# A fused block-causal attention and gated FFN kernel: the second batch's v loads ahead of the casts of w_out, a new order in tiles 0 to 2, and the last tile's stores on two queues

## The chip, the cores and the metric

The kernel runs on one core of a Trainium2 chip. The time is the device time of one execution in microseconds (us); lower is better. Before the change the median of three runs is 353.19 us (352.29 to 354.38).

The core's engines run their own instruction streams in program order: PE multiplies matrices, DVE (VectorE) and ACT (ScalarE) work element by element, POOL (GpSimd) does that too and here issues the loads that change the type on the way, and SP (SyncE) only issues transfers. Semaphores order the engines among each other.

## The reference

```python
# q, k, v: (8 batches, 8 heads, 576 positions, 64); blocks of 64 positions
scores = q @ k.T / sqrt(64)          # per batch and head
scores = where(block(i) >= block(j), scores, -1e9)
attn = softmax(scores) @ v
x = attn, as 4608 tokens x 512       # heads side by side
gate = maximum(x @ w_gate, 0)        # 512 x 1536
out = (gate * (x @ w_val)) @ w_out   # 1536 x 512, result float32
```

## The kernel before, in words

**Tiles.** The FFN runs in nine tiles of 512 tokens: tile j below 8 holds the first 512 positions of batch j, and tile 8 the last 64 positions ("tails") of all eight. A tile multiplies x by w_gate and w_val (L1193; 96 matmuls), ACT applies the maximum (L1204), DVE multiplies the two (L1214), and the result goes through w_out: in tiles 0 and 1 by 48 plain matmuls (L1298), from tile 2 on by seven products of half blocks (`seven_products`, L891), for which POOL forms sums of w_out's blocks (`weight_sums`, acts W0 to W5). In the last tiles a similar scheme serves the first stage too (L1063).

**Attention** runs in rounds: round r = 4b + p handles heads 2p and 2p + 1 of batch b, so rounds 4 to 7 are the second batch's. A round has the scores (act `s4`; L552), the exponentials on ACT (`e4`; L557), zeros for the masked corners (`c4`), the products with v for its two heads (`a4` and `b4`; ten L687 matmuls each), and the transpose of the result into the FFN's x (`x4`; L730). For the tails there are acts `S`, `L`, `E`, `A` and `B` by batch.

**Order.** PE's stream is the FFN's generator, `ffn_gen`, which yields once per matmul. All else is an "act" with a name and a place in the table `AT`, counted in yields of the FFN: 0 to 95 is the first stage of tile 0, 96 to 143 its w_out, 144 on tile 1, 288 on tile 2. The end of the kernel sorts the acts by place, runs the FFN up to each place, and then issues the act:

```python
for n in sorted(acts, key=lambda n: AT[n]):
    at = int(place_of(AT[n]))
    ffn(at - place[0])
    place[0] = max(place[0], at)
    acts[n]()
```

No scheduler moves anything after that, so the order in the table is the order on every engine. The table's base stands at L1454, and blocks of `AT.update` further down replace places. `HOW` (from L1687) says which engine does what.

**The second batch's entry.** q, k and v come by these acts, and all of them share POOL, SP and the transfers' bandwidth with the load of w_out:

- SP loads q and k of four heads at a time in float32 (`E1q0`, then `E1q4` for q and `E1q6` for k of heads 4 to 7; `load_wide`, L164), and w_out in six pieces of 512 KB (`w00` to `w21`; `load_w`, L458).
- POOL casts q and k to bf16 (`q0`, `q4`, `q6`; L174) and most of w_out (`cw00` to `cw21/0`; L484). The last pieces of w_gate and w_val are cast by `cg21`, `cv21/0` and `cv21/1` in the same way.
- v is loaded by POOL's queue with the cast on the way: `E1v0` to `E1v3`, two heads each, two transfers each (`load_v_casting`, L186; the DMA at L183). Before the change, POOL's order was: `cg21`, `cv21/0`, `q0`, `E1v0`, the six w_out casts, `E1v1`, `q4`, `q6`, `E1v2`, `E1v3`.
- PE transposes q and k of heads 4 to 7 in act `m2` (`pe_wide`, 8 + 8 matmuls at L367), and ACT or DVE copies them out by head pair (`m2`, `m3`). Round 6 needs this.
- The third batch's q and k come over a DMA transpose and are put in order by `u0` to `u3` (`unpermute`, L330); its v by `E2v0` to `E2v3`.

**Stores.** A tile's result is kept in blocks of 256 columns and stored by `put_block`. In the last tile each block is two transfers, i = 0 and 1 (L773); its four blocks come in the order (0,0), (1,256), (0,256), (1,0), the last in two halves p0 = 0 and 1, where the first number is the half of the batches and the second the first column.

Of the kernel before, what the change touches and what calls it, by code (L numbers as in the profile page):

```python
# [17 lines left out]
def kernel(  # L18
# [10 lines left out]
    nc = tc.nc  # L29
# [729 lines left out]
    def put_block(j, hi, n0, ob, p0, p1):  # L759

        n = slice(n0, n0 + 256)
        rows = ob.rearrange("q (p n) -> q p n", n=256)
        if j < B:
            r0 = S * j + 256 * hi + 128 * p0
            (nc.scalar if j < UPS - 1 else nc.sync).dma_start(
                out[r0 : r0 + 128 * (p1 - p0), n].rearrange("(p q) n -> q p n", q=128),
                rows,
            )
        else:
            by_batch = out.rearrange("(b s) n -> b s n", b=B)  # L770
            for i in range(2):
                b0 = 4 * hi + 2 * p0 + i
                ((nc.scalar, nc.sync)[i] if (hi, n0) == (1, 0) else nc.sync).dma_start(  # L773
                    by_batch[b0 : b0 + 2 * (p1 - p0) - 1 : 2, 512:576, n].rearrange(
                        "b s n -> s b n"
                    ),
                    rows[64 * i : 64 * i + 64],
                )
# [91 lines left out]
    def seven_products(j, quads, sums, late_up=None, head=None):  # L870
# [42 lines left out]
        def store_later(hi, n0, ob, p0=0, p1=2):  # L913
            if store:
                store.pop()()
            if j < B:
                store.append(lambda: put_block(j, hi, n0, ob, p0, p1))
            else:
                put_block(j, hi, n0, ob, p0, p1)
# [440 lines left out]
    dve, act, pool = nc.vector.tensor_copy, nc.scalar.copy, nc.gpsimd.tensor_copy  # L1360
# [7 lines left out]
    with tc.manual_schedule(engines={E.PE, E.DVE, E.Activation, E.Pool, E.SP}):  # L1368
# [4 lines left out]
        def round_at(r, how):  # L1373

            exps = []

            def begin():
                exps.extend(visit(r))
                exps[0]()
                exps[1]()  # L1380

            corner, first, second, xT = how
            return {
                f"s{r}": begin,
                f"e{r}": lambda: exps[2](),
                f"c{r}": lambda: corners(r, zeros_by[corner]),
                f"a{r}": lambda: head_av(r, 0, first),
                f"b{r}": lambda: head_av(r, 1, second),
                f"x{r}": lambda: (
                    to_xT_pe(r, by[xT[0]], xT[1]) if xT else to_xT_dma(r)  # L1390
                ),
            }
# [53 lines left out]
        def mains_1(hp):  # L1446
# [7 lines left out]
        AT = {  # L1454
            "Lq0": -63.5,
            "Lq2": -62.27,
            "Lv0": -61.59,
            "Lv2": -59.5,
            "Lq6": -59.5,
            "Lq4": -59.5,  # L1460
            "v00": -58.48,
            "g00": -56.5,
# [224 lines left out]
        HOW = {  # L1687
            "t0": ("act", "dve"),
            "t1": ("dve", "dve"),
            "m0": (("act", "dve"), ("sc", "ffn")),  # L1690
            "m1": (("dve", "act"), None),
            "m2": (("act", "act"), ("sc", "ffn")),
            "m3": (("act", "act"), None),
            "u0": ("pool", "pool"),
            "u1": ("dve", "dve"),
# [95 lines left out]
                "cv00/23": "pool",  # L1791
            }
        )
        STEADY = {"s": 2, "e": 8, "c": 15, "a": 22, "b": 26, "x": 26.1}
        acts = {
            "Lq0": lambda: e0.load_qk(0, 2, nc.scalar),
# [85 lines left out]
        for b in range(4, B):  # L1882
            base = 144 * (b - 1)
            for i in range(4):
                r = 4 * b + i
                here = ("sc", "sc") if i == 3 else ("one", "ffn")
                acts.update(round_at(r, ("dve", *here, None)))
                for n, p in STEADY.items():
                    AT[f"{n}{r}"] = base + 28 * i + p + (5 if i == 3 and n in "abx" else 0)
# [17 lines left out]
        for c in range(6):  # L1907
# [268 lines left out]
                "cg00/23": -17.37,  # L2176
                "c3a": -3.24,
                "cg01/23": 4.15,
            }
        )  # L2180
        assert set(acts) == set(AT), set(acts) ^ set(AT)
# [43 lines left out]
```

## Time and profile before

| | |
|---|---|
| median of three runs | 353.19 us (352.29 to 354.38) |
| the profiled execution's own time | 352.44 us |
| its span in the profile | 350.7 us |
| time outside the span | 1.74 us |
| w_out loads: issue to landing, median | 10.6 us |
| busy share POOL, ACT, DVE | 51%, 57%, 60% |

How to read it: the profile comes from one execution, whose span is the time from its first to its last recorded instruction; the execution's own time is 1.74 us more. Engines are shown as PE (matmuls), PEld (PE's loads of weights), DVE, ACT, POOL and SP; an ending "q" stands for the issue of transfers. A line such as "L687" is a line of the kernel. In a timeline a row is a run of like instructions with its start and length, and in brackets the idle time just before it and what ended it. The chain of waits follows the work that ended last back to what released it, and so names one releaser where several may have come at nearly the same time. A row of a window holds the busy time of the engines in that stretch, the granted clock of PE, the busy share of the transfer engines and the rate in GB/s. Landing is when a transfer's data are there.

### The profile page before, as it was taken

The page shows a single profiled execution, that of the slowest core. Times are in us where ns is not written, and L with a number is a line of the kernel's source. Part 1 is how long each engine was busy: PE and PEld are TensorE (multiplying, and loading weights), DVE is VectorE, ACT ScalarE, POOL GpSimd, SP SyncE. Part 2 cuts the span into 40 slices and gives each one's busy share as a digit, 9 for nine tenths or more (in the row PEclk, how much of TensorE's full clock was granted, in tenths as well). Part 3 has the DMA queues.
Part 4 walks back from the last instruction along what each step waited for, and adds up shares of the span by engine and source line. Part 5 has one row for each costly group of instructions (what it writes and reads, how often), then busy time and mean ns, then how long its engine had stood idle before and what let it go on. Part 6 is the DMA issues. An engine that isn't in the chain of part 4 may idle for free.

```text
span 350.7 us, 8432 instructions
## 1 busy us (share of the span) xinstructions
PE 341.3 (97%) x3317; PEld 216.4 (62%) x3317; DVE 210.4 (60%) x541; ACT 200.3 (57%) x323; POOL 178.2 (51%) x216
## 2 busy tenths in 40 slices
PE   7899999999999999999999999999999999999994
PEld 3544445555554568555855576556755598888883
DVE  4654435557538675466636762666456757787783
ACT  4942776888336672666365555655366627725731
POOL 4836798799709910690029209950490042711630
PEclk9999999999999999999999999999999999999999
DMA  8999999999989999999449953999410012003005
GB/s 243 294 354 374 348 269 176 136 92 145 161 199 104 133 172 176 136 148 165 73 111 139 136 114 112 132 141 147 119 47 15 17 49 96 3 3 119 2 3 120
DMA packets 155624, 48.40 MB, mean 138 GB/s; under 512 B 134592, under 2 KB 152000, under 8 KB 155584
## 3 DMA queue, kind: packets, MB, share of 16 engines
q0 software_dynamic: 83776, 10.49, 57.8%
q1 hardware_dynamic: 65872, 30.68, 39.5%
q10 hardware_dynamic: 5936, 6.69, 6.1%
q8 instruction: 26, 0.43, 0.6%
q14 instruction: 14, 0.11, 0.1%
HBM read 37.75 MB, written 9.44 MB: 135 GB/s over the span
## 4 chain that ended last, share of the span: by engine, by line
PE 83%; DMA 10%; DVE 2%; ACT 2%; POOL 1%; issue 0%; SPq 0%; POOLq 0%; DVEq 0%
PE ffnp L1193 36%; PE ffnp L891 12%; PE upa L1063 6%; PE one L891 5%; DMA stage<-in_moe_w_val_dram 5%; PE ffnp L1298 4%; DMA stage<-in_moe_w_out_dram 3%; PE sc L552 3%; PE upc L1063 3%; PE ffnp L687 2%; PE one L552 2%; DMA v_bf<-in_v_dram 2%; ACT attnT L516 2%; PE ffnp L1063 1%; PE one L687 1%; PE sc L687 1%
## 5 line engine op out<-in xcount | busy, mean ns | idle before, releaser
L1214 DVE TENSOR_TENSOR hT<-gate_sb,ffnp 128x512 bf16<-128x512 bf16 x82 | 55.9, 683 | 60.7 <-ACT gate_sb L1204 31.7
L1193 PE MATMUL ffnp<-xT,wv 128*128 128x512 bf16 x328 | 90.0, 379 | 0.0
L1193 PE MATMUL ffnp<-xT,wg 128*128 128x512 bf16 x316 | 86.4, 379 | 0.0
L1204 ACT ACTIVATE gate_sb<-ffnp 128x512 bf16<-128x512 f32 x79 | 48.2, 613 | 41.9 <-PE ffnp L1193 41.7
L557 ACT ACTIVATE attnT<-sc 128x1024 bf16<-128x1024 f32 x56 | 57.7, 1047 | 0.0
L1193 PEld LDWEIGHTS <-wv 128*128 128x128 bf16 x336 | 30.2, 98 | 33.6 <-issue 3.0
L1193 PEld LDWEIGHTS <-wg 128*128 128x128 bf16 x336 | 30.8, 98 | 32.2 <-issue 2.2
L439 POOL DMA_DIRECT2D q_bf<-in_q_dram x20 | 17.7, 900 | 37.8 <-DVE hT L1214 36.8
L923 ACT COPY ob<-ffnp 128x512 f32<-128x512 f32 x21 | 12.3, 586 | 41.9 <-PE ffnp L891 40.4
L891 PEld LDWEIGHTS <-stage 128*128 128x128 bf16 x336 | 32.5, 98 | 3.7
L687 PEld LDWEIGHTS <-attnT 128*128 128x128 bf16 x640 | 26.9, 98 | 12.4 <-issue 1.5
L439 POOL DMA_DIRECT2D v_bf<-in_v_dram x30 | 24.3, 879 | 10.7 <-DVE stage L802 10.1
L891 PEld LDWEIGHTS <-hT 128*128 128x128 bf16 x252 | 24.1, 98 | 4.6 <-DVE hT L1095 0.7
L1298 PE MATMUL ffnp<-wo,hT 128*128 128x512 bf16 x96 | 23.8, 379 | 0.0
L564 ACT ACTIVATE attnT<-one 128x512 bf16<-128x512 f32 (+1 forms) x28 | 15.1, 540 | 14.7 <-PE ffnp L552 14.6
L552 PEld LDWEIGHTS <-kTm 64*128 64x128 bf16 x384 | 13.0, 94 | 14.2 <-issue 9.0
L891 PE MATMUL ffnp<-wo,hT 128*128 128x256 bf16 x168 | 21.5, 273 | 0.1
L891 PE MATMUL ffnp<-stage 128*128 128x256 bf16 x168 | 21.3, 273 | 0.0
L439 POOL DMA_DIRECT2D k_bf<-in_k_dram x20 | 18.0, 944 | 0.0
L848 DVE TENSOR_TENSOR stage<-hT 128x512 bf16<-128x512 bf16 (+1 forms) x45 | 17.5, 393 | 0.5
L552 PE MATMUL sc<-qTm,kTm 64*128 64x512 bf16 (+1 forms) x168 | 17.7, 305 | 0.0
L1099 POOL TENSOR_TENSOR hT<-attnT,gate_sb 128x512 bf16<-128x512 f32 x4 | 4.6, 1159 | 25.1 <-ACT gate_sb L1107 25.1
(186 smaller groups left out, 628.9 us busy)
## 6 DMA issues: line engine op xcount, KB each, us to landing
out_dram<-ob ACTq DMA_DIRECT2D x24, 256.0 KB, 2.4
stage<-in_moe_w_val_dram SPq DMA_DIRECT2D x6, 512.0 KB, 8.2
stage<-in_moe_w_gate_dram SPq DMA_DIRECT2D x6, 512.0 KB, 8.6
stage<-in_moe_w_out_dram SPq DMA_DIRECT2D x6, 512.0 KB, 10.6
q_bf<-in_q_dram POOLq DMA_DIRECT2D x20, 128.0 KB, 4.6
k_bf<-in_k_dram POOLq DMA_DIRECT2D x20, 128.0 KB, 5.8
v_bf<-in_v_dram POOLq DMA_DIRECT2D x20, 128.0 KB, 6.2
stage<-in_q_dram SPq DMA_DIRECT2D x4, 512.0 KB, 10.1
```

The source lines that it names most:

```text
L439: ins = nc.gpsimd.dma_start(dst, part_of)
L552: nc.tensor.matmul(o, kTm[b % 2][head_of(hh), c, hp, :], qT, start=True, stop=True)
L557: return lambda: nc.scalar.activation(at[:, :, lo : lo + 512], sc, AF.Exp, scale=scale)
L564: nc.scalar.activation(at[:, hh, 1024 : 1024 + w], third[hh][:, 0:w], AF.Exp, scale=scale)
L687: nc.tensor.matmul(av[:, p, :], at[:, col : col + 128], v_bf[b % 2][:, c, h, :], start=(p == 0), stop=(c == p), skip_group_check=True,)
L848: ins = (eng or nc.vector).tensor_tensor(out=s(i), in0=a, in1=b, op=op)
L891: nc.tensor.matmul(to, sums.of(c)[which]()[:, 128 * p : 128 * p + 128], right, start=first, stop=(c == 5), skip_group_check=True,)
L1063: nc.tensor.matmul(to[:, 256 * f : 256 * f + 256], left(which, u // 2)[:, kc, lo : lo + 128], right[which](kc), start=new and (f, kc) == ( ...
L1193: ins = nc.tensor.matmul(to, (wg, wv)[t][f // 4][:, c, 128 * (f % 4) : 128 * (f % 4) + 128], x[:, c], start=(c == 0), stop=(c == 3),)
L1204: nc.scalar.activation(gate_sb, gate, AF.Relu)
L1214: nc.vector.tensor_tensor(out=h, in0=gate_sb, in1=val, op=AX.mult)
L1298: ins = nc.tensor.matmul(op, hT[f][:, 128 * s : 128 * (s + 1)], wo[f // 4][:, f % 4, n0:n1], start=(f == 0), stop=(f == 11),)
```

## The change

- In `put_block`, the last tile's transfers are given out anew: block (0,0) and the second half of (1,0) wholly to SP, of the others i = 0 to SP and i = 1 to ACT. SP issues seven instead of eight, ACT three instead of two.
- In `HOW`, the copies of `u0` and `u1`, which were on POOL and ACT, DVE and POOL, go to DVE and ACT, DVE and DVE, and `cw21/1` from ACT to DVE.
- In `AT`, some ninety places are new. On the engines this comes to:
  - POOL: `cv21/0` ahead of `cg21`; `E1v0` and `E1v1` both ahead of the w_out casts (`E1v2` and `E1v3` stay behind `q6`); the tails' loads `T0` ahead of `T1`; the third batch's v in the order of heads 6 and 7, 2 and 3, 4 and 5, 0 and 1, in a row (before: 2, 3, 0, 1, 6, 7, 4, 5 with a copy of `u1` between); the second `weight_sums` ahead of the load `l3`.
  - PE: `s4` two places later and `s5` one earlier; `m2` ahead of `b4` and `a4`, which before stood ahead of it, and `b4` ahead of `a4`; in tile 1 the tail products `A1` behind `s8`, the tail acts `S2` and `L2` of the third batch some places earlier, `x11` later; the others by one or two places.
  - SP: the DMA transpose `dq3` ahead of `x8`.

The diff, cut to the edits that these lines speak of:

```diff
-                ((nc.scalar, nc.sync)[i] if (hi, n0) == (1, 0) else nc.sync).dma_start(
+                (nc.scalar if i and (hi, n0) != (0, 0) and not p0 else nc.sync).dma_start(
...
+        HOW.update(
+            {
+                "cw21/0": "pool",
+                "cw21/1": "dve",
+                "t0": ("act", "dve"),
+                "u0": ("dve", "act"),
+                "u1": ("dve", "dve"),
+            }
+        )
...
+                "E1v1": 32.255,
+            }
+        )
+        AT.update(
+            {
+                "E1q0": 30.6,
...
+                "cv21/0": 32.13,
+                "w21": 34.31,
+                "E1q6": 34.34,
+                "E1q4": 34.34,
+                "cg21": 34.35,
+                "q0": 34.39,
+                "E1v0": 35.95,
+                "E1v1": 35.95,
+                "cw00": 36.0,
+                "cw01": 36.0,
+                "cw10": 36.01,
+                "cw11": 36.03,
+                "cw21/0": 36.05,
+                "cw20": 36.05,
+                "E2q4": 37.3,
+                "q4": 41.12,
+                "cv20": 44.31,
+                "q6": 48.64,
+                "E1v2": 88.39,
+                "s4": 96.02,
...
+                "T0": 108.36,
...
+                "s5": 115.76,
...
+                "T1": 119.45,
+                "m2": 122.13,
+                "E0v": 122.62,
+                "b4": 122.95,
+                "a4": 123.23,
...
+                "m3": 125.27,
+                "s6": 128.0,
...
+                "b5": 130.73,
...
+                "E2v3": 177.42,
+                "E2v2": 178.09,
+                "E2v1": 178.09,
+                "S1": 181.62,
+                "E2v0": 182.84,
+                "s8": 199.54,
+                "e8": 200.02,
+                "A1": 202.39,
+                "W1": 205.95,
+                "l3": 206.44,
...
+                "b8": 215.84,
...
+                "dq3": 246.36,
+                "e11": 246.48,
+                "a10": 248.52,
+                "x8": 249.37,
...
+                "S2": 269.46,
+                "W5": 271.62,
+                "L2": 279.14,
+                "x11": 280.4,
...
```

More of the change, by code (lines that the diff above doesn't have):

```diff
@@ L2178 @@
                 "cg01/23": 4.15,
+                "E1v1": 32.255,
[4 more added lines that the diff above has]
+                "E1q0": 30.6,
+                "w01": 30.61,
+                "w00": 30.76,
+                "w11": 30.82,
+                "w20": 30.83,
+                "w10": 30.83,
+                "cv21/0": 32.13,
[18 more added lines that the diff above has]
+                "s4": 96.02,
+                "e4": 96.84,
+                "T0": 108.36,
+                "c4": 112.71,
+                "s5": 115.76,
+                "e5": 117.58,
+                "T1": 119.45,
[3 more added lines that the diff above has]
+                "a4": 123.23,
+                "o0": 123.74,
+                "c5": 124.54,
+                "m3": 125.27,
+                "s6": 128.0,
+                "e6": 128.26,
+                "a5": 129.94,
+                "b5": 130.73,
+                "E2q0": 132.8,
+                "c6": 135.35,
+                "x4": 135.54,
+                "x5": 135.83,
+                "s7": 137.1,
+                "a6": 138.8,
+                "e7": 141.05,
+                "b6": 141.36,
+                "o1": 141.79,
+                "t0": 163.05,
+                "E0": 168.0,
+                "L0": 171.03,
+                "T2": 175.24,
+                "u2": 176.91,
+                "E2v3": 177.42,
[8 more added lines that the diff above has]
+                "l3": 206.44,
+                "s9": 208.21,
+                "c8": 208.52,
+                "e9": 212.62,
+                "t2": 214.9,
+                "b8": 215.84,
+                "s10": 223.76,
+                "B1": 224.54,
+                "u3": 228.36,
+                "W2": 228.46,
+                "e10": 229.53,
+                "c9": 230.18,
+                "a8": 230.33,
+                "b9": 230.89,
+                "a9": 233.34,
+                "E2v4": 234.75,
+                "s11": 242.93,
+                "W3": 245.35,
+                "c10": 245.88,
+                "dq3": 246.36,
+                "e11": 246.48,
+                "a10": 248.52,
+                "x8": 249.37,
+                "c11": 250.92,
+                "b10": 253.86,
+                "a11": 256.77,
+                "b11": 256.86,
+                "x9": 258.07,
+                "W4": 265.15,
+                "x10": 267.44,
+                "S2": 269.46,
+                "W5": 271.62,
+                "L2": 279.14,
+                "x11": 280.4,
+                "d3": 280.48,
+                "E2": 292.1,
+                "lv3": 298.84,
+                "l4": 318.55,
+                "D4": 338.16,
```

## The prediction

> **What bounds the kernel now.** First the page: the busy shares, then the granted clock in slices of the span.
>
> ```profile
> span 350.7 us, 8432 instructions
> PE 341.3 (97%) x3317; PEld 216.4 (62%) x3317; DVE 210.4 (60%) x541; ACT 200.3 (57%) x323; POOL 178.2 (51%) x216
> ...
> PEclk9999999999999999999999999999999999999999
> ```
>
> PE is busy 341.3 of 350.7 us at a full clock, and the change neither adds nor removes a matmul. So only three things can be won: PE's few waits, the work before its stream runs, and the stores after its last matmul. And anything that makes PE wait is lost to the end, since PE has no idle time later in which to make it up.
>
> Next, where PE waits. The list of PE's waits from 24 to 60 us has a single row, and the chain of waits shows what lies behind it:
>
> ```profile
> PE ffnp L687 <- DMA v_bf<-in_v_dram: 0.4, 1, 0.4
> ```
> ```profile
> 33.17 11.34 DMA stage<-in_moe_w_out_dram
> ...
> 44.56 0.61 POOL wo L484
> ...
> 45.85 6.77 DMA v_bf<-in_v_dram
> ...
> 52.67 0.48 PE ffnp L687 x10
> ```
>
> POOL casts w_out (L484) until 45.17, only then issues the last pair of E1v1 (heads 2 and 3 of the second batch), and PE's round 5 starts at 52.67 on their landing. This is the wait that the change takes away. Its neighbourhood, from PE's timeline:
>
> ```profile
> 41.08 4.74 PE L1298 MATMUL ffnp<-wo,hT 128*128 128x512 bf16 x20
> ...
> 47.28 0.47 PE L687 MATMUL one<-v_bf,attnT 128*128 128x65 bf16 x10
> 47.58 0.59 PE L1298 MATMUL ffnp<-wo,hT 128*128 128x512 bf16 x2
> 48.01 0.47 PE L687 MATMUL ffnp<-v_bf,attnT 128*128 128x65 bf16 x10
> ...
> 48.53 0.61 PE L367 MATMUL sc<-ident,q_bf 128*128 128x128 bf16 x8
> 49.10 0.62 PE L367 MATMUL ffnp<-ident,k_bf 128*128 128x128 bf16 x8
> 49.56 1.46 PE L1298 MATMUL ffnp<-wo,hT 128*128 128x512 bf16 x6
> ...
> 51.91 0.38 PE L1298 MATMUL ffnp<-wo,hT 128*128 128x512 bf16 x1
> 52.67 0.48 PE L687 MATMUL ffnp<-v_bf,attnT 128*128 128x65 bf16 x10 [0.37 <-DMA v_bf<-in_v_dram]
> ```
>
> A row's time runs to the modelled end of its last matmul; starts of back-to-back L1298 matmuls lie about 0.215 us apart (two matmuls from 47.58 to 48.01). So the wait is 52.67 - (51.91 + 0.215) = 0.54 us. The second row of interest is 49.10, the transposes of k (act m2): eight of them take 0.46 us to the next start (49.10 to 49.56), which from 48.53 would be 48.99, so PE waited 0.11 us there too. POOL's timeline says on what:
>
> ```profile
> 32.74 0.61 POOL L484 CAST wv<-stage 128x512 bf16<-128x512 f32 x1 [0.38 <-DMA stage<-in_moe_w_val_dram]
> ...
> 35.23 1.69 POOL L183 DMA_DIRECT2D v_bf<-in_v_dram  x2
> 38.46 2.03 POOL L484 CAST wo<-stage 128x1024 bf16<-128x1024 f32 x2 [1.54 <-DMA stage<-in_moe_w_out_dram]
> 41.25 3.01 POOL L484 CAST wo<-stage 128x1024 bf16<-128x1024 f32 x3 [0.76 <-DMA stage<-in_moe_w_out_dram]
> 44.56 0.61 POOL L484 CAST wo<-stage 128x512 bf16<-128x512 f32 x1 [0.31 <-DMA stage<-in_moe_w_out_dram]
> 45.12 1.48 POOL L183 DMA_DIRECT2D v_bf<-in_v_dram  x2
> ...
> 48.01 1.04 POOL L174 CAST k_bf<-stage 128x1024 bf16<-128x1024 f32 x1 [0.36 <-DMA stage<-in_k_dram]
> ```
>
> The cast of k waits for k's landing (just before 48.01) and ends at 49.05; PE starts on it at 49.10. The chain of waits names v alone, but k is a bound nearly as tight, and one that no work on PE can pass. That is the heart of what follows.
>
> **The change part by part.**
>
> *E1v1 ahead of the casts.* Its two issues (1.48 us) go from 45.12 to about 37. POOL idled 1.54 us ahead of 38.46, so they fit there, and the first w_out cast is late by 0.1 us at most, which the idle 0.76 us ahead of 41.25 takes up. v lands long before round 5: PE's 0.54 us go. **-0.54.**
>
> *What E1v1 then runs beside.* Its bytes, formerly moved when SP's loads were nearly through, now follow E1v0's at once, beside the q and k loads of the second head group that m2 needs. What such a pair costs the loads is in the windows: E1v0's pair is in flight from some point after 39 until 45.99 (issued at 35.23 and 36.17, the slower one landing 9.8 us after).
>
> ```profile
> 38.00:39.00 1.00, 1.00 (x6) 0.44 (x5) 1.00 (x3) 1.00 (x2) 0.54 (x1) 1.00 1.05 387
> 39.00:40.00 1.00, 1.00 (x7) 0.31 (x7) 0.60 (x2) 0.31 (x2) 1.00 (x2) 1.00 1.10 373
> 40.00:41.00 1.00, 1.00 (x11) 0.50 (x11) 0.00 (x0) 1.00 (x4) 0.49 (x1) 1.00 1.22 313
> 41.00:42.00 1.00, 1.00 (x7) 0.45 (x5) 0.65 (x1) 1.00 (x2) 0.75 (x1) 1.00 1.21 318
> 42.00:43.00 1.00, 1.00 (x6) 0.43 (x5) 0.03 (x1) 0.79 (x1) 1.00 (x2) 1.00 1.32 289
> 43.00:44.00 1.00, 1.00 (x6) 0.41 (x5) 0.00 (x0) 0.00 (x0) 1.00 (x2) 1.00 1.32 281
> 44.00:45.00 1.00, 1.00 (x6) 0.46 (x5) 0.00 (x0) 0.47 (x1) 0.69 (x2) 1.00 1.30 292
> 45.00:46.00 1.00, 0.98 (x7) 0.30 (x7) 0.14 (x1) 0.15 (x1) 1.00 (x3) 1.00 1.12 370
> ```
> ```profile
> DMA to landing us min/median/max: 2.6/4.7/9.8
> ```
>
> The last column (GB/s) falls from 387 to 281-292 and is back at 370 where the pair comes through. From 39 to 46 it sums to 2236 against 7 x 387 = 2709: 473 KB short, and 131 KB of what moved was v itself (two heads of 128x4x64 in two bytes). So the loads lost 473 to 604 KB, 1.2 to 1.6 us at 387 GB/s. A second pair of the same shape costs the same for a load that stands behind all of it, and less for k, which need not outlast it all. The trace holds no case of E1v1 beside k, so 0 is one end and 1.6 the other; I take **1.2 us**, the nearest row's lower value.
>
> The Trainium skill, "DMA: Bandwidth & Descriptors", "Queues, rings and completion order", says that a DMA engine goes round the queues that have work, one packet each; by that rule small v packets would take every second turn from the loads, which speaks against this move. The fall in the last column agrees with it; taken to the end, turn by turn, it would put k at the upper 1.6 us and the time, as an estimate, at 354.8 instead of 354.4.
>
> *m2 ahead of b4 and a4.* Before, PE has two visits of ten L687 (0.30 us each, 47.28 to 47.58) and one L1298 (0.215) between 47.70 and 48.53 that now stand behind m2: PE comes to m2 at about 47.70. With k landing 1.2 us later, its cast ends at 50.25 and the k transposes start at 50.30 instead of 49.10, with 0.30 + 0.30 + 0.215 = 0.83 us of work still to do behind them. By then q, landing earlier and cast first, is no limit. So PE is 1.2 + 0.83 = **+2.03** late at round 6's scores. Round 5's products, formerly ready to start at 52.13, stand at 54.16 instead of 52.67: **+1.49** with the 0.54 us already taken off.
>
> *E1v2, E1v3* are still issued behind the k cast, so 1.2 us later, and PE's use of them is 1.5 us later: nothing. *cg21 behind cv21/0*: its cast (1.0 us, as the w_out casts of the same shape) ends at 34.4, where PE's matmuls with it stood at 34.2 in PE's timeline: 0.2 us of waiting. But 41.08 to 45.56 would do for twenty L1298 in a row (19 x 0.215 + 0.38 = 4.47) where the row has 4.74: 0.27 us of waiting, for the last casts of w_out, whose load does not move. A PE that comes 0.2 us later waits 0.2 us less there: nothing, at worst +0.2.
>
> *u0, u1: two copies from POOL to DVE; second batch's v in the order 6,7 / 2,3 / 4,5 / 0,1.* The rows:
>
> ```profile
> L330 DVE COPY kTm<-perm x1: 636/636/636, 69.8 to 69.8; 128x512 bf16<-128x512 bf16 x1
> ```
> ```profile
> 69.90 4.61 POOL L183 DMA_DIRECT2D v_bf<-in_v_dram  x6
> ...
> 75.45 1.55 POOL L183 DMA_DIRECT2D v_bf<-in_v_dram  x2
> ```
> ```profile
> 80.35 0.47 PE L687 MATMUL ffnp<-v_bf,attnT 128*128 128x65 bf16 x10
> ```
> ```profile
> DMA to landing us min/median/max: 2.8/4.2/7.2
> ```
>
> DVE gets two copies, about 1.3 us, and is idle 40% of the span: nothing. Heads 0 and 1 are now issued last: shifted by 1.49 us, eight issues of 0.77 us from 71.39 put the last at 76.8, its landing (median 4.2) at 81.0, and round 8 needs it at 80.35 + 1.49 = 81.84: nothing, 0.8 us to spare. The other reorderings of tiles 0 to 2 move acts by a few places among matmuls that wait for nothing: 0, with 0.3 either way.
>
> *The stores of the last tile.*
>
> ```profile
> 342.81 5.36 SPq L773 DMA_DIRECT2D out_dram<-ob  x8
> ```
> ```profile
> 344.61 0.69 DVE L927 TENSOR_TENSOR ob<-one,ob 128x512 f32<-128x512 f32 x1 [0.56 <-PE one L891]
> ```
>
> SP issues eight in one run of 0.67 us each, and the fifth, of the block that DVE ends at 345.30, cannot go before 342.81 + 4 x 0.7 = 345.6. With one of the second pair on ACT it goes at 345.36, and four follow from there in both kernels: **-0.3** (0 to -0.6).
>
> **Sum:** +1.49 - 0.3 = +1.2 on the profiled execution's 352.44, which is 353.64. That execution lies 0.75 below the median of the runs shown, 353.19, so 354.4 on that footing. (Half a per cent, 1.77 us, is about what a measurement of this kernel can tell from no change.)
>
> **The rivals.**
>
> 1. *k is not late.* E1v1's transfers slip between the loads. For it: before, k still had E1v1's pair issued at 45.12 beside its last two microseconds. Then m2's k part starts at 49.10 as before, with 0.83 behind it: +0.83 - 0.54 - 0.3 = 0.0: 353.2. Chance 0.24.
> 2. *The v wait comes back a batch later* (slower). Heads 0 and 1 are now the last of eight issues, and if their landing takes the 7.2 us seen at most and not 4.2, they land at 84.0, 2.2 us after round 8's need; the price begins where landing takes over 5 us. 354.4 + 2.2 = 356.6, down to 354.7 near the threshold. Against it: nothing waited for v there before, and POOL is free of two copies. Chance 0.18.
> 3. *Only the gains* (faster). k arrives earlier than before, since E1v1 no longer runs beside its end, far enough that m2 waits for nothing: -0.54 - 0.11 - 0.3: 352.2, and 351.9 with the stores at -0.6. Against it: the cast that k waits for ends no sooner than 48.01 + 1.04 unless k lands 0.9 us earlier. Chance 0.08.
>
> **How the numbers follow.** The forecast has 0.50, and its own range is k's delay from 0.8 to 1.6, the stores from 0 to -0.6 and 0.3 for the small orders: 353.6 to 355.2. Faster by over 0.5% means below 351.4, which no sum here reaches: 0.07 for what I overlook. Slower means above 354.96: 0.12 of the forecast, 0.15 of rival 2, a little besides: 0.29. Within: 0.64. The range leaves out the far end of rival 2 and the near end of rival 3: 352.2 to 356.2.
>
> **What would show it.** Right: POOL's k cast starting near 49.2 and not 48.0; PE's k transposes (L367, ffnp) near 50.3 with idle of about 2 us around m2; no wait at round 5; the same number of PE gaps after 60 us; SP's last L773 issue some 0.3 us sooner after the last matmul. Wrong: k cast at 48.0 (rival 1), an L687 waiting for v near 82 (rival 2), or m2 without a wait (rival 3).

## The result, and the profile after

The changed kernel takes 355.0 us in the median of 22 runs (353.5 to 357.44) beside 352.93 for the kernel before on the same chips (22 runs, 352.29 to 357.77). The ratio is 1.0044, with a 95% interval of 1.0024 to 1.0064: slower by a little under half a per cent, inside the range of the prediction and on its side. Nine of the changed kernel's runs lie between 353.5 and 353.88 and the rest from 354.54 up, while thirteen of the kernel before lie between 352.29 and 353.19. The profiled execution took 353.67 us where the sum said 353.64. Part of that agreement is luck: two terms were off in opposite directions, and a further cost, which this one execution does not contain, lies between it and the median.

First the list of PE's waits over the whole span of the kernel after. The columns are the waiting group, what it waited for, the sum in us, the number of times and the longest.

```profile
PE ffnp L367 <- POOL k_bf L174: 1.4, 1, 1.4
...
PE sc L687 <- DVE attnT L1363: 0.3, 1, 0.3
```

The wait of round 5 for v is gone. In its place stand one for the cast of k, and a short one at round 9 for zeros that DVE writes. POOL's timeline of the kernel after has the new order, and the k cast late:

```profile
32.91 0.62 POOL L484 CAST wv<-stage 128x512 bf16<-128x512 f32 x1 [1.75 <-DMA stage<-in_moe_w_val_dram]
33.46 1.04 POOL L484 CAST wg<-stage 128x1024 bf16<-128x1024 f32 x1
...
35.63 3.18 POOL L183 DMA_DIRECT2D v_bf<-in_v_dram  x4
38.77 2.06 POOL L484 CAST wo<-stage 128x1024 bf16<-128x1024 f32 x2
...
44.59 0.87 POOL L484 CAST wo<-stage 128x512 bf16<-128x512 f32 x1 [0.18 <-DMA stage<-in_moe_w_out_dram]
46.77 1.04 POOL L174 CAST q_bf<-stage 128x1024 bf16<-128x1024 f32 x1 [1.31 <-DMA stage<-in_q_dram]
48.88 1.04 POOL L174 CAST k_bf<-stage 128x1024 bf16<-128x1024 f32 x1 [1.07 <-DMA stage<-in_k_dram]
```

All four v issues stand in one row of 3.18 us ahead of the w_out casts. POOL now sits idle ahead of both later casts, for 1.31 and 1.07 us: it is the loads that are late, not POOL. PE's timeline of the kernel after shows the price:

```profile
47.99 0.61 PE L367 MATMUL sc<-ident,q_bf 128*128 128x128 bf16 x8
49.98 0.62 PE L367 MATMUL ffnp<-ident,k_bf 128*128 128x128 bf16 x8 [1.38 <-POOL k_bf L174]
50.44 0.47 PE L687 MATMUL ffnp<-v_bf,attnT 128*128 128x65 bf16 x10
50.96 0.47 PE L687 MATMUL one<-v_bf,attnT 128*128 128x65 bf16 x10
...
53.83 0.47 PE L687 MATMUL ffnp<-v_bf,attnT 128*128 128x65 bf16 x10
```

PE stands at m2's q part at 47.99, does it at once, and then has nothing to do until 49.98; b4 and a4, which could have filled 0.6 us of that, come behind. Round 5's second product, which waited for v before, starts at 53.83 instead of 52.67.

Why k is late is in the windows of the kernel after (the last column is GB/s):

```profile
38.00:39.00 1.00, 1.00 (x7) 0.43 (x5) 0.92 (x2) 0.92 (x3) 1.00 (x3) 1.00 1.04 385
...
44.00:45.00 1.00, 1.00 (x6) 0.49 (x5) 0.43 (x1) 0.00 (x0) 0.82 (x2) 1.00 1.35 274
45.00:46.00 1.00, 0.98 (x8) 0.27 (x7) 0.31 (x2) 0.00 (x0) 0.46 (x1) 1.00 1.33 275
46.00:47.00 1.00, 1.00 (x11) 0.43 (x8) 0.10 (x1) 0.81 (x3) 0.23 (x1) 1.00 1.37 274
47.00:48.00 1.00, 1.00 (x7) 0.41 (x6) 0.83 (x2) 1.00 (x2) 0.81 (x1) 1.00 1.33 277
48.00:49.00 1.00, 0.60 (x9) 0.42 (x7) 0.45 (x1) 1.00 (x2) 0.12 (x1) 1.00 1.36 270
```

Before, the rate was back at 370 in the window from 45, and it stayed high while k came in:

```profile
46.00:47.00 1.00, 1.00 (x11) 0.41 (x6) 0.85 (x3) 0.87 (x3) 1.00 (x2) 1.00 1.09 385
47.00:48.00 1.00, 1.00 (x15) 0.60 (x13) 0.52 (x1) 1.00 (x2) 0.64 (x1) 1.00 1.08 350
```

Now it stays at 270 to 277 until 49, for as long as the second pair of v moves. The packets between 46 and 47, by queue (q1 is SP's, q0 is POOL's; number, MB, share of the time), first of the kernel before and then of the kernel after, show who moves:

```profile
q1 hardware_dynamic: 383, 0.39, 109.1%
```
```profile
q1 hardware_dynamic: 251, 0.24, 89.1%
q0 software_dynamic: 249, 0.03, 48.2%
```

Before, none of v's packets moved in that stretch, although POOL had issued both loads of E1v1 by 46.60. After, v has as many packets in it as SP's loads, of some 120 bytes against some 960 (0.03 MB by 249 and 0.24 MB by 251), and SP's queue moves 0.24 MB in the microsecond instead of 0.39.

The second new wait, on PE's timeline of the kernel after:

```profile
86.15 0.47 PE L687 MATMUL one<-v_bf,attnT 128*128 128x65 bf16 x10
86.90 0.48 PE L687 MATMUL sc<-v_bf,attnT 128*128 128x65 bf16 x10 [0.28 <-DVE attnT L1363]
```

and on DVE's timeline of the kernel after, what those zeros (L1363) queue behind:

```profile
85.95 0.66 DVE L330 COPY qTm<-perm 128x512 bf16<-128x512 bf16 x1
86.68 0.30 DVE L1363 MEMSET attnT<- 64x128 uint32 x2
```

The copy is u3, which the change moves from place 217 to 228, right ahead of round 9's zeros (c9, 230.18). Ten L687 take 0.30 us, so the second product would have started at 86.45; the row says 86.90, a loss of 0.45.

The end, SP's timeline of the kernel after:

```profile
344.36 5.04 SPq L773 DMA_DIRECT2D out_dram<-ob  x7
```

It starts 1.55 later than before (342.81) and ends at 349.40 against 348.17, 1.23 later: the stores won 0.32. The same ledger by position: PE's last matmul starts at 347.15 against 345.60, 1.55 later, of which 1.15 to 1.16 were there at round 5 and at the entry of tile 1, and 0.4 come at round 9.

### The profile page after: what moved, and what is told of

It reads as the page before. It is cut to its first block, busy times and chain, and to the rows that moved or that the text cites. A ratio compares the mean times of both kernels' runs of the same rounds, so it can differ in the third digit from the quotient of the medians.

```text
span 351.9 us, 8390 instructions
## 1 busy us (share of the span) xinstructions
PE 338.3 (96%) x3277; PEld 215.8 (61%) x3317; DVE 212.0 (60%) x544; ACT 200.3 (57%) x322; POOL 177.2 (50%) x214
## 4 chain that ended last, share of the span: by engine, by line
PE 83%; DMA 10%; DVE 2%; issue 1%; ACT 1%; POOL 1%; SPq 0%; DVEq 0%; POOLq 0%
PE ffnp L1193 37%; PE ffnp L891 11%; PE upa L1063 6%; DMA stage<-in_k_dram 5%; PE one L891 5%; PE ffnp L1298 4%; PE sc L552 3%; PE upc L1063 3%; PE ffnp L687 2%; PE one L552 2%; DMA stage<-in_moe_w_val_dram 2%; DMA stage<-in_v_dram 2%; PE one L687 2%; PE ffnp L1063 1%; DMA xT<-xnat 1%
## 5 line engine op out<-in xcount | busy, mean ns | idle before, releaser
L1193 PE MATMUL ffnp<-xT,wv 128*128 128x512 bf16 x308 | 87.1, 379 | 1.3 <-issue 0.6
L1193 PE MATMUL ffnp<-xT,wg 128*128 128x512 bf16 x302 | 83.5, 379 | 1.1 <-issue 0.3
L687 PEld LDWEIGHTS <-attnT 128*128 128x128 bf16 x640 | 27.0, 98 | 11.7 <-issue 1.3
L1298 PE MATMUL ffnp<-wo,hT 128*128 128x512 bf16 x90 | 22.7, 379 | 0.3 <-issue 0.2
```

The costliest lines, as they stand in the source:

```text
L687: nc.tensor.matmul(av[:, p, :], at[:, col : col + 128], v_bf[b % 2][:, c, h, :], start=(p == 0), stop=(c == p), skip_group_check=True,)
L1193: ins = nc.tensor.matmul(to, (wg, wv)[t][f // 4][:, c, 128 * (f % 4) : 128 * (f % 4) + 128], x[:, c], start=(c == 0), stop=(c == 3),)
L1298: ins = nc.tensor.matmul(op, hT[f][:, 128 * s : 128 * (s + 1)], wo[f // 4][:, f % 4, n0:n1], start=(f == 0), stop=(f == 11),)
```

## The experiments

### The parts of the change one by one

Four kernels ran once each, with a profile. The first three undo one part of the changed kernel each; the fourth adds one part to the kernel before.

```diff
# after_v1_behind: on the changed kernel
+        AT.update({"E1v1": 36.055})
# after_m2_behind: on the changed kernel
+        AT.update({"b4": 122.05, "a4": 122.08})
# after_u3_early: on the changed kernel
+        AT.update({"u3": 217.23})
# before_v1_ahead: on the kernel before
+        AT.update({"E1v1": 32.26})
```

**after_v1_behind.** 

> The changed kernel with E1v1 alone back behind the w_out casts (place 36.055). Theory (v's small packets beside the q and k loads make k late): POOL's k cast starts near 48.0 again instead of 48.88, PE's k transposes near 49.1 instead of 49.98, so round 5 and all that follows come 0.8 to 0.9 us sooner; v then lands near 52.9 and round 5's second product, which would come up at 52.95, waits 0 to 0.3 us. PE's last matmul starts at 346.3 to 346.6 instead of 347.15. Rival (k is late for another reason, such as the new order of the loads or of the casts): the k cast stays at 48.9, and the time is the same or, with the v wait back, longer.

POOL's and PE's timelines:

```profile
48.09 1.04 POOL L174 CAST k_bf<-stage 128x1024 bf16<-128x1024 f32 x1 [0.16 <-DMA stage<-in_k_dram]
```
```profile
49.19 0.62 PE L367 MATMUL ffnp<-ident,k_bf 128*128 128x128 bf16 x8 [0.59 <-POOL k_bf L174]
...
53.04 0.47 PE L687 MATMUL ffnp<-v_bf,attnT 128*128 128x65 bf16 x10
```

With v alone back in its place the k cast comes back to 48.09, the transposes of k to 49.19, and round 5's second product to 53.04, 0.79 sooner, without a wait for v. At round 15's scores PE is at 140.07 against 140.90 in the changed kernel, 0.83 sooner. So v's place makes k late, by about 0.8 us, and the rest of the order by no more than 0.1 (48.09 against 48.01 in the kernel before). The last matmul, however, started at 348.40 and the execution took 354.96 us, longer than the changed kernel's profiled one. That was not expected, and the next part is about it.

**after_m2_behind.** 

> The changed kernel with b4 and a4 back ahead of m2. Theory (m2's k transposes wait for the k cast whatever PE has done before): PE comes to m2 0.6 us later, its wait for k falls from 1.38 to about 0.8 us, the k transposes stay at 49.98, and round 6 and the rest come 0.6 us sooner: last matmul near 346.55. Rival (order does not matter, since the products of round 4 wait themselves): the wait moves to b4 or a4 and the last matmul stays at 347.15.

The k transposes start at 49.87, with 0.76 us of idle time ahead of them instead of 1.38. Round 15's scores come at 140.18, 0.72 sooner. What PE does ahead of the wait is free: the expected 0.6 and a little more (0.1 of it is the k cast, at 48.77). The profile names zeros of DVE as the end of this wait, but the k cast ends at 49.81, 0.06 ahead of the transposes, as far as it does in the changed kernel (49.92 and 49.98), so the wait is read as k's.

**after_u3_early.** 

> The changed kernel with u3 back at its former place 217.23. Theory (DVE's copy of u3 stands ahead of round 9's corner zeros, on which PE's round 9 products wait at 86.90): that wait of 0.28 us in the list of PE's waits is gone, and the last matmul starts 0.4 us sooner, near 346.75. Rival (the wait comes from the third batch's v or from the copies moved to DVE): the wait stays, the last matmul at 347.15.

The wait on L1363 is gone from the list. Round 15's scores come at 140.29, 0.61 sooner, of which 0.16 were there at round 6 already (52.28 against 52.44); the remaining 0.45 are u3's. The copies moved to DVE stayed where they were in this run, so it was not they.

**before_v1_ahead.** 

> The kernel before with E1v1 alone moved ahead of the w_out casts. Theory: the k cast starts near 48.9 instead of 48.0, PE's k transposes at 49.9 to 50.0 with a wait of 0.9 to 1.0 us, and round 5 no longer waits for v: +0.88 - 0.54, so the last matmul near 345.95 instead of 345.60. Rival (v ahead is a gain by itself and the loss is all in the order of m2): k cast at 48.0, last matmul near 345.06.

The k cast starts at 48.87, the k transposes at 49.97 after 0.82 us of idle time, and round 5's second product at 52.99 against 52.67: it loses 0.32. The last scores of the batch (round 15) come at 139.66 against 139.34, again 0.32. The forecast said 0.34 from 0.88 - 0.54. Moving v ahead, by itself, costs more at k than it saves at v.

### A wait that comes and goes at tile 3

In all four the execution was longer than the ledger up to round 15 allows. PE's timeline of after_v1_behind has the place:

```profile
144.22 0.38 PE L1193 MATMUL ffnp<-xT,wg 128*128 128x512 bf16 x1 [1.91 <-DMA xT<-xnat]
```

and SP's timeline of it shows what the awaited transfer stood behind:

```profile
125.60 7.38 SPq L448 DMA_TRANSPOSE kTm<-k_bf  x1
...
135.68 3.39 SPq L736 DMA_TRANSPOSE xT<-xnat  x2
139.16 1.20 SPq L673 DMA_TRANSPOSE xTt<-xtail  x1
140.41 11.89 SPq L736 DMA_TRANSPOSE xT<-xnat  x2
```

Tile 3's first stage needs the fourth batch's last xT transpose (the first of the two that start at 140.41). Ahead of it SP issues a transpose of the tails that only the last tile wants (L673). In the kernel before the same row of L736 starts at 138.24, and PE does not wait. In the changed kernel's profiled execution it starts at 140.38, as late as here, and PE does not wait either. It comes to the place 0.84 us later than here, so part of what an edit wins ahead of this place is lost at it. That alone is not enough for the 1.91 us: in the profiles of before and of the changed kernel the transfer landed 2.5 us after its issue, and in the four variants 3.4 to 4.0 us after (3.8 here). Why the landing differs is not shown. The other three waited 1.1 to 2.7 us in all for transposes of this row. How late SP's run of transposes comes differs from profile to profile too: the issue of the k transposes ahead of it (L448) took 6.40 us in the profile of before and 7.33 to 7.64 in those of the changed kernel and of after_v1_behind and before_v1_ahead. So an edit was made that takes one transpose out of the way, and tried on both kernels, with repeated runs:

```diff
# after_tail_last, after_three_tail: on the changed kernel
# before_stores_tail, before_stores_tail_E2late: on the kernel before, with the change's put_block
-        if x is not None and h == 7:
-            tail_to_xT(b, xtails[b])
...
             xnat.rearrange("p c n -> p (c n)"),
         )
+        if hp == 3 and b in xtails:
+            tail_to_xT(b, xtails[b])
# after_three_tail also
+        AT.update({"b4": 122.05, "a4": 122.08, "u3": 217.23})
+        HOW.update({"cw21/1": "act"})
# before_stores_tail_E2late also
+        AT.update({"E2q4": 122.5})
```

**after_tail_last.** 

> The changed kernel; in each batch from the fourth on the transfer that transposes the tails (SP L673, wanted only in the last tile) goes behind the batch's last xT transpose and not ahead of it. In four variants PE waited 1.0 to 1.9 us at tile 3's first L1193 for that last xT transpose, which SP issued only when L673 was through. Theory (that wait is what the many longer executions of this kernel hold, and SP's queue causes it): the last xT transpose issues 1.2 us sooner, the wait shrinks by up to 1.2 us or is gone, the median falls from 355.0 to 353.6 to 354.2. Rival (the wait hangs on the landing times of the transfers, not on SP's order): the xT transpose lands as late as before and the median stays near 355.

Median 353.71 us (12 runs, 353.51 to 354.75), ratio to the kernel before 1.0013 [0.9996, 1.003]. The fastest run is as fast as the changed kernel's (353.5), and the longest, which was 357.44 there, is 354.75. SP's timeline:

```profile
135.09 4.95 SPq L734 DMA_TRANSPOSE xT<-xnat  x3
140.13 1.20 SPq L673 DMA_TRANSPOSE xTt<-xtail  x1
```

Three xT transposes now stand in one run, and the last is issued ahead of L673, at 138.7 instead of 140.38. It landed 3.2 us after its issue, later than the 2.5 of the changed kernel's profile, and PE still did not wait. So what lies between the changed kernel's profiled 353.67 and its median of 355.0 is, for the most part, this wait; this is read from the medians, since no long execution of the changed kernel has a profile.

**after_three_tail.** 

> The same, and three parts of the change undone as well: b4 and a4 ahead of m2, u3 at 217.23, cw21/1 on ACT; E1v1 stays ahead of the casts. Theory: 0.6 to 0.8 from m2 and 0.4 to 0.6 from u3 come off, and POOL's cast of cw21/0 lasts 0.61 again instead of 0.87 us: PE's last matmul, where tile 3 does not wait, near 345.9 instead of 347.15, and the median 352.4 to 353.2, about that of the kernel before. Rival (the parts cover each other): a gain of only the larger one, 353.0 to 353.8.

Median 352.86 (352.6 to 353.8), ratio 0.9992 [0.9975, 1.001]: the kernel before, to within the measurement. The last matmul started at 346.59, not 345.9: in this profile PE waited 0.4 us for the cast cg21, which took 1.24 us, and the k cast started at 49.22, later than in the changed kernel. The medians fall from 353.71 to 352.86, by 0.85 us, which is more than the larger part alone (0.72) and less than the 1.17 of both (0.72 and 0.45). With intervals of 0.17% either way on each ratio, this favours the theory that the parts add and does not prove it. POOL's timeline of this run has the cast that had been 0.87 in the changed kernel:

```profile
44.91 0.61 POOL L484 CAST wo<-stage 128x512 bf16<-128x512 f32 x1 [0.26 <-DMA stage<-in_moe_w_out_dram]
```

**before_stores_tail.** 

> The kernel before with the change's new stores of the last tile and the tails' transpose behind the xT transpose. Theory: 0.3 us from the stores, and the longer executions lose up to 1.2 us: median 352.0 to 352.5 against 352.9. The last SP store is issued 1.65 to 1.75 us after the last matmul starts, and not 2.02. Rival (the stores gain nothing alone): ratio 1.000.

Median 352.5 (352.09 to 353.6), ratio 0.998 [0.9963, 0.9997]. SP's row of L773 starts at 342.79 and lasts 5.05 us, so it ends 0.33 sooner than before with the last matmul at the same 345.58: the stores are worth 0.3 us alone too. The ratio is worth 0.7 us; that its rest is the tail transpose is argued from the narrower spread of the runs, not shown apart.

**before_stores_tail_E2late.** 

> The same with the second half of the third batch's q and k loads (E2q4, two loads of 512 KB, needed near 61 us) tied to a matmul near 48 us instead of following the second batch's k at once. Theory (v's landing at 52.6 is set by what shares the transfers between 46 and 52.6): v of round 5 lands 1 us or more sooner and its wait of 0.54 us goes, without k being late: last matmul near 345.1, median 351.5 to 352.0, below both kernels. Rival (the landing is set by POOL's issue at 45.1 to 46.6 alone): v still lands near 52.6 and the wait stays.

Median 352.29 (351.93 to 353.51), ratio 0.9967 [0.9949, 0.9986]: it beats both kernels, by an interval that ends below 1. PE's timeline of it, at round 5:

```profile
49.04 0.61 PE L367 MATMUL ffnp<-ident,k_bf 128*128 128x128 bf16 x8
...
52.05 0.47 PE L687 MATMUL ffnp<-v_bf,attnT 128*128 128x65 bf16 x10
```

Neither k nor v is waited for, although POOL issues v where it did before (45.17): with the two loads of E2q4 (512 KB each) no longer behind k in SP's queue, 588 of the 616 packets between 47 and 48 are POOL's, where before_stores_tail has none of POOL's among 363. But 0.3 us come back as a wait for k's tails (L397), the last matmul starts at 345.58 and not 345.1, and the step from 352.5 to 352.29 is less than the intervals can tell.

### Two attempts to go on from there

```diff
# on before_stores_tail: best_E2_last
+        AT.update({"E2q4": 131.6})
# on before_stores_tail: best_mid
+        AT.update({"E1v1": 32.34, "cw20": 103.0, "cw21/0": 110.83})
+        HOW.update({"cw20": "act", "cw21/0": "dve"})
# best_mid_E2_last: both
```

**best_E2_last.** 

> The kernel before with the new stores and the tails' transpose behind, and E2q4 last of the third batch's loads, tied to a matmul near 53 us (the run before had it near 48 us, where v came in time but PE then waited 0.3 us for k's tails at L397). Theory (that wait came from E2q4 running beside the tails' loads): no wait for v and none at L397; last matmul near 345.0 to 345.3, median 352.0 to 352.2. Rival (E2q4 is then late itself): waits of PE or ACT behind 60 us, median over 352.5.

The kernel before took 354.17 us in the median beside these three, so their ratios and not their times are to be compared with the others. Median 355.2, ratio 1.0031 [1.0007, 1.0055]. The theory fell: the waits at the tails grew instead of going. Its list of PE's waits:

```profile
PE ffnp L397 <- DMA k_bt<-in_k_dram: 1.3, 1, 1.3
...
PE ffnp L391 <- DMA q_bt<-in_q_dram: 0.9, 1, 0.9
```

v was in time (round 5's second product at 52.24, no wait), but now the loads of 512 KB move beside the tails' loads of the first two batches, which PE needs soon after, and 2.2 us go there.

**best_mid.** 

> The kernel before with the new stores and the tails' transpose behind, the casts of w_out's last two pieces on ACT (cw20) and DVE (cw21/0), and E1v1 on POOL right behind the fourth w_out cast, some 2 us sooner than before but not ahead of all casts. Theory (v shares with k from the moment it moves, and only the part before k's landing costs): v's issues near 43.3 to 44.8, k cast 0 to 0.5 us late, no wait for v, the wait at the last w_out casts shorter; last matmul 344.9 to 345.5. Rival (any v ahead of k costs what it saves): k cast near 48.8, last matmul 345.8 or later.

Median 352.85, ratio 0.9973 [0.9953, 0.9994]; the intervals do not separate it from before_stores_tail. Both theory and rival were wrong about v: POOL issued it at 43.27, some 1.85 us sooner, k was on time (cast at 48.02), and yet PE waited for v as before:

```profile
52.82 0.48 PE L687 MATMUL ffnp<-v_bf,attnT 128*128 128x65 bf16 x10 [0.52 <-DMA v_bf<-in_v_dram]
```

With E2q4 in its old place v lands at about the same time whether issued at 43.3 or 45.1. All 385 packets between 46 and 47 are SP's here too, and the first of this pair's come in the window from 47, over 4 us after the issue. So v starts late, and is not only slow; what holds it back was not tried.

**best_mid_E2_last.** 

> Both together. Theory: as best_mid with nothing added, since v no longer needs the room, 0 to 0.2 us sooner. Rival: the two gains add, median under 351.8.

Median 355.47, ratio 1.0051 [1.0021, 1.0081]. No wait for v here, but 2.3 us at L391: the cost of E2q4's place, without a gain beside it. Neither expectation held.

## Why the prediction was right, and where not

- *Round 5's wait goes, 0.54:* right; it is in no list of the kernel after.
- *E1v1 makes k late, 1.2 us (0 to 1.6):* right in kind, too large. The cast starts 0.87 later, 48.88 against 48.01, the transposes of k 0.88 later, and 0.8 of it comes back when v alone is moved back. The 1.2 was what a whole pair costs a load that stands behind all of it; k, as the working itself said, need not outlast the pair, and the nearest row's lower value should have been cut for that. What the prediction held for rival 1, that k had E1v1's pair beside its last two microseconds in the kernel before, was misread: no packet of v moved between 46 and 47 there, so k came in alone before and with v beside it after. The upper 1.6, for turns taken evenly to the end, was too large although the turns are even (251 and 249): 124 packets of v still moved between 49 and 50, when k had landed.
- *m2 ahead of b4 and a4, +0.83:* right: undoing b4 and a4 alone gave 0.72, of which 0.1 was the earlier k cast.
- *Round 5 comes at +1.49:* +1.16 measured, which is 0.88 + 0.83 - 0.54 to within 0.01. The term mis-sized is k's.
- *cg21 behind cv21/0, nothing:* right at the end, but not by the cover named. PE did wait 0.2 us for the cast, but the wait for w_out later shrank by under 0.1 us, since POOL's cast of cw21/0 took 0.87 instead of 0.61 us. What hid both was the wait for k.
- *The other reorderings, 0 with 0.3 either way:* wrong by 0.45, and the step that failed. u3's copy was costed by place among PE's matmuls, not by what queues behind it on DVE; round 9's zeros do, and PE waits for them.
- *u0, u1 and v of the third batch, nothing:* no wait of the kernel after stands there, so rival 2 did not occur.
- *The stores, -0.3:* -0.32 in the profile, -0.33 alone.
- *The sum, +1.2 on the profiled execution:* 353.67 against 353.64. k's term was 0.33 too large, the order of DVE 0.45 too small, and the rest is rounding. That the two errors nearly cancelled is luck.
- *The median:* forecast 354.4 from an execution's offset of 0.75. The offset left out that the kernel has a wait whose length differs from profile to profile (tile 3's first xT), which the profile of before did not contain and which no view of it names. It is the likely reason why the measured 1.0044 is more than the profile's 353.67 / 352.44 = 1.0035. That the same wait makes the longer runs of the kernel before is argued from before_stores_tail's narrower spread, not shown in a profile of one of them.

## What to carry to other kernels

Where the chain of waits names one transfer, look for the others on which there is almost no slack (here k, on which PE waited 0.11 us) and which share the transfers: moving the named one ahead takes its time from them, and here 0.88 us at k were paid for 0.54 at v. Taking unneeded bytes out of the stretch (the two loads of E2q4) freed v for 0.3 us of waiting elsewhere, but the loads must go somewhere where nobody waits either, as the attempts that moved them too late show. And a single profile of a kernel whose runs spread by some microseconds may lack the wait that its median holds: profile a few variants, and compare at a fixed place in the program and not at the end.

## What the runs showed that was not expected

Of a cast on DVE and one on POOL at the same time, the later one takes longer. In the changed kernel DVE's timeline has

```profile
33.51 1.27 DVE L484 CAST wv<-stage 128x512 bf16<-128x512 f32 x1
...
44.56 0.43 DVE L484 CAST wo<-stage 128x512 bf16<-128x512 f32 x1 [2.92 <-DMA stage<-in_moe_w_out_dram]
```

At 44.59, just behind DVE, POOL's cast of the same shape starts and takes 0.87 us; with the DVE cast on ACT again it took 0.61. At 33.51 it is the other way round: DVE starts just behind POOL's cast of w_gate (33.46, 1.04 us), and takes 1.27 us where the same cast took 0.42 in the kernel before, with POOL idle:

```profile
33.36 0.42 DVE L484 CAST wv<-stage 128x512 bf16<-128x512 f32 x1
```

The Trainium skill, "SBUF — State Buffer", "Who interferes with whom", describes a port pair that DVE and GpSimd hold in turn for a whole instruction. Both rows agree with it but for 0.14 us: POOL's cast ends 0.47 us behind DVE's, of 0.61 that it takes alone, and DVE's ends 0.28 behind POOL's, of 0.42.
